# Attention scores of two batches on two halves of the array's rows, inside an attention + two-layer kernel

## The chip, the cores and the metric

The kernel runs on one core of one Trainium2 chip. The core has TensorE (PE in the views, its weight loads are PEld), VectorE (DVE), ScalarE (ACT), GpSimd (POOL) and SyncE (SP, which issues the DMAs here). The metric is the device time of one execution in microseconds (us), as the median of several executions; less is better. All matrix inputs arrive in HBM; the program is one launch.

## The reference, cut to what matters

```python
batch, n_heads, seq, head_dim = 4, 8, 576, 64
# attention, per batch and head
scores = matmul(q, k.T) / 8                       # 576 x 576
cum    = cumsum(maximum(s, 0))                    # one number per key / query
scores = where(causal, -1e9, scores + minimum(-(cum[query] - cum[key]), 0))
attn   = exp(scores - max) / (sum + 1e-9)
x      = attn @ v                                 # 2304 tokens x 512
# layer 1: (x @ w_a) * (x @ w_b) @ w_out          # d_ff 1536
# layer 2: relu(x @ w_in) ** 2 @ w_out2           # d_ff 2048
```

Below the diagonal `-(cum[query] - cum[key])` is never above zero, so the minimum changes nothing there, and the term in `cum[query]` is the same for a whole row, which the softmax removes. What the kernel adds to a score is therefore `cum[key]` alone. The weights are 64-bit floats, which the kernel takes apart into 32-bit parts itself.

## The kernel before, in words

The program first lists its operations and then orders them itself. `Plan.order` (line 148) is a list scheduler: for each engine it holds the operations whose inputs are planned to be there, takes the one that can start first in planned time, and of several the one with the lowest rank (stream, then the order in which they were listed). Costs are written beside each operation, a lateness per engine is added to its result (`LATE`, line 81), and a tile of a tag with few buffers waits in planned time until one is free. What comes out is a fixed order for each engine; on the chip each engine takes its instructions in that order and waits on semaphores. So an operation that is late holds everything behind it on its engine.

Streams in use here: `first` (attention of batch 0), `moe` (layer 1), `next` (attention of batch 1, listed among layer 1's steps from step `TURN` on), `att` (attention of batches 2 and 3), `late` and `fill` (40 dummy matmuls named `glow`, which the planner puts where TensorE would idle; a bank's first matmul may also get a few dummy ones, `idle`, shown as `st<-warm`).

Attention of a head (`softmax`, line 586): the 576 queries are five blocks of 96 or 120 rows; with the causal mask the scores of a head are six pieces of 96, 216, 336, 456, 288 and 288 columns (the last block's 576 keys are cut in two). `banks` (line 499) puts these six into four PSUM banks, and each bank is one planned TensorE operation. In batches 0 and 1 (`WHOLE = 2`) a piece is one plain 32-bit product, contracted over 65 rows: 64 rows of the head, and row 64 that holds ones in the queries' tile and `cum` of that head in the keys' tile, so that the sum comes along in the same product:

```python
both = ((tq[: D + 1, qc], tk[: D + 1, ks]),)
cost += 4 * kn / 2.4 + 13
```

The trace shows two matmul records for each such product. In batch 0 the causal mask is added by a small bf16 product (`tri`) into the same bank. Then for each piece DVE reduces to the row's maximum (`neg`), ACT takes the exponential (`e`) and frees the bank. After both heads of a pair `weigh` (line 669) transposes the weights on TensorE (`pt`), copies them, and multiplies by the values (`av`): there the two heads of a pair lie in two halves of the array's columns (`"tile_position": (0, h * D)`, line 719), and the calls go head 0, head 1 by turns.

Banks: the tag `s` has 2 buffers and serves scores; in batch 0 the third and fourth bank of a head come from the tag `mm` (3 buffers), which layer 1 uses for its products (`ab`, `py`).

Loads: `load_first` (line 436) brings the keys and queries of a head into rows 0 to 63 of two tiles (tags `T2k` and `T2q`, 2 buffers each), `prep_first` (line 533) then loads `cum` of the head into row 64 by a small DMA and scales the queries by 1/8. At the start `cum` is made by DVE (maximum, scan), and its rounded part `ch` and remainder `cl` are written to HBM (`cd`) for batches 2 and 3. Those batches use other operands (`prep`, line 547), a piece there is two products in the faster 32-bit format of the array (`F32R`).

Around this: layer 1 on tokens 0 to 511 (chunk 0) needs batch 0 alone, its steps run beside the attention of batch 1, and at the same time its weights are loaded and taken apart (`split_w`, `words`, `decode`: tiles `roomxh`, `roomxl`, `words`, `wh`, `wl`) and written back to HBM (`wlab`, `wlo`).

Of the kernel before, what the change touches and what calls it, by code (L numbers as in the profile page):

```python
# [263 lines left out]
def attention_moe_moe(tc, q, k, v, s, w_a, w_b, w_out, w_in2, w_out2, out):  # L264
# [21 lines left out]
    MORE = 3 * NF1  # L286
    TURN = 4
    LF1 = 6
# [244 lines left out]
    def prep_first(b, p):  # L533

        load_values(b, p)
        heads = []
        for hh in (2 * p, 2 * p + 1):
            if (b, hh) not in first_k:
                load_first(b, hh)
            tk = first_k[b, hh]  # L540
            dma(tk[D : D + 1].part("c"), cum[b * H + hh : b * H + hh + 1], 2)
            tq = first_q[hh % 2]
            scaled(S, tq[:D].part("x"))
            heads.append((tq, tk))
        return heads
# [40 lines left out]
    def softmax(b, p, h, head, one):  # L586
# [7 lines left out]
        for blk, (tag, width, off) in places.items():  # L594
            if tag not in tiles:
                tiles[tag] = at([P, -(-width // 32) * 32], F32, tag, 3, f"{tag}{nm}")
            place[blk] = (tiles[tag], off)
        for i, pieces in enumerate(banks):
            ps = mm_bank(f"st{nm}_{i}") if b == 0 and i % 4 > 1 else bank(f"st{nm}_{i}")
            off = 0  # L600
            calls, cost, got = [], 0, []
            for blk, k0, kn in pieces:
                at_, m = kb[blk]
                qc = slice(at_, at_ + m)
                to = ps[:m, off : off + kn]
                diag = at_ >= k0 and at_ + m <= k0 + kn
                ks = slice(k0, k0 + kn)
                if b < WHOLE:
                    tq, tk = head
                    both = ((tq[: D + 1, qc], tk[: D + 1, ks]),)  # L610
                    cost += 4 * kn / 2.4 + 13
                else:
                    t1, t2q, t2k = head
                    both = ((t1[:66, 0, qc], t1[:66, 1, ks]), (t2q[:, qc], t2k[:, ks]))
                    cost += 2 * (kn / 2.4 + 15)
                calls += [("matmul", (to, *ab), {"stop": True}) for ab in both]
                if diag and b < MASKED:
                    tri = mask[:m, EDGE : EDGE + m]
                    calls.append(("matmul", (to[:, kn - m :], plain[:m, :m], tri), {"stop": True}))
                    cost += 70  # L620
                e, eo = place[blk]
                got.append((blk, k0, m, to, kn, diag, e[:m, eo + k0 : eo + k0 + kn]))
                off += kn
            if b < WHOLE:
                ins = [tq.part("x"), tq.part("c"), tk.part("x"), tk.part("c")]
# [5 lines left out]
            for z, (_, _, kw) in enumerate(calls):  # L631
                kw.update(start=z == 0, skip_group_check=z > 0)
            pe(cost, calls, ps, ins)
            if b == 0 and i == 0 and hh in (0, 2):
# [11 lines left out]
            held += got  # L646
            whole = [x for x in held if x[0] != LAST or pieces[0][0] == LAST]
            held = [x for x in held if x not in whole]
            if pieces[0][0] == LAST:
# [19 lines left out]
    def weigh(b, p, places, chunk, u):  # L669
# [6 lines left out]
        for i, keys in enumerate(key_banks):  # L676
            m = kb[keys[0]][1]
            rights = []
            for h, place in enumerate(places):
                ps = bank(f"pt{nm}_{h}_{i}", "t")  # L680
                calls, ins, off, spans = [], [ident], 0, []
                for j in keys:
                    k0, _ = kb[j]
                    c0 = max(k0, g0)
                    for blk in range(j, len(kb)):
                        at_, mq = kb[blk]
                        if g0 <= at_ < g0 + n:
                            e, eo = place[blk]
                            ins += [e.part((blk, x)) for x in ((0, HALF) if blk == LAST else (0,))]
                            col = off + at_ - c0  # L690
# [909 lines left out]
```

## Time and profile before

| | |
|---|---|
| Time, median of 3 executions | 1019.21 us (1017.22 to 1020.49) |
| Profiled execution | 1023.91 us, its span 1022.1 us |
| PE busy | 1002.8 us (98% of the span), 5612 matmul records |
| DVE, ACT, POOL busy | 735.5, 603.9, 322.3 us |
| DMA | 240.58 MB, 235 GB/s on average |
| Granted TensorE clock | 1.00 in nearly every stretch |

Stages, read from the names in the timeline: 0 to 10 us set-up; 10 to 62 us attention of batch 0; 62 to 206 us attention of batch 1 beside layer 1's chunk 0; 206 to 378 us attention of batches 2 and 3 beside layer 1; then layer 1 and layer 2 alone. Matmuls are pipelined: the records' durations contain their latency and overlap, so the price of one is read from the distance between starts, not from its duration.

### The profile page before, as it was taken

How to read it: one execution, taken by the hardware profiler on the slowest of the kernel's cores; microseconds unless marked ns; L12 is line 12 of the kernel's file. 1: busy time of each engine (PE TensorE's matmuls, PEld its weight loads, DVE VectorE, ACT ScalarE, POOL GpSimd, SP SyncE). 2: the span in 40 equal slices, each digit the busy share in tenths (PEclk: the TensorE clock that was granted, in tenths of full speed). 3: DMA queues.
4: the chain of work that ended last, by engine and by line, in shares of the span. 5: the costliest groups of instructions: out<-in, count | busy, mean ns of one | idle time of the engine just before them, and what ended most of it. 6: DMA issues, size and time to landing. Idle time of an engine off the chain costs nothing.

```text
span 1022.1 us, 16764 instructions
## 1 busy us (share of the span) xinstructions
PE 1002.8 (98%) x5612; PEld 867.8 (85%) x5619; DVE 735.5 (72%) x1546; ACT 603.9 (59%) x1373; POOL 322.3 (32%) x293
## 2 busy tenths in 40 slices
PE   9999999999999999999999999999999999999997
PEld 5766777777777778788889999999999999999997
DVE  5878876756677765565697898688767755876566
ACT  6777886565777643343344544487565766657552
POOL 2243134325454622101122323323335212431123
PEclk9999999999999999999999999999999999999999
DMA  7458896558778667857666668499968876678664
GB/s 226 131 157 256 273 288 186 152 150 258 228 199 246 185 212 262 275 183 233 206 207 207 208 206 273 164 336 363 344 219 322 313 260 231 246 273 319 220 233 165
DMA packets 138006, 240.58 MB, mean 235 GB/s; under 512 B 21320, under 2 KB 91072, under 8 KB 137920
## 3 DMA queue, kind: packets, MB, share of 16 engines
q1 hardware_dynamic: 137920, 239.52, 71.1%
q8 instruction: 44, 0.72, 0.3%
q14 instruction: 42, 0.34, 0.1%
HBM read 181.42 MB, written 52.11 MB: 228 GB/s over the span
## 4 chain that ended last, share of the span: by engine, by line
PE 75%; DMA 5%; DVE 2%; SPq 1%; ACT 1%; issue 0%; DVEq 0%; ACTq 0%
PE ab L261 14%; PE pa L261 9%; PE py L261 8%; PE po_0t L261 6%; PE pw L261 5%; PE pc L261 5%; PE wa L261 4%; PE st L261 3%; PE av L261 3%; PE pt L261 3%; PE wc L261 2%; PE pb L261 2%; PE po_2b L261 2%; PE po_1b L261 2%; PE po_0b L261 2%; PE po_3b L261 2%
## 5 line engine op out<-in xcount | busy, mean ns | idle before, releaser
L261 ACT ACTIVATE e<-st,neg 120x336 f32<-120x336 f32 (+2 forms) x192 | 93.5, 492 | 28.5 <-DVE neg L261 26.6
L261 PE MATMUL py<-g,wh 128*128 128x512 f32 x288 | 92.0, 401 | 1.4 <-DVE y L261 1.2
L261 PE MATMUL ab<-xh,wh 128*128 128x512 f32 x192 | 77.4, 403 | 0.0
L261 PE MATMUL ab<-xh,lo 128*128 128x512 f32 x192 | 75.0, 391 | 0.0
L261 PE MATMUL ab<-xl,wh 128*128 128x512 f32 x192 | 75.0, 390 | 0.0
L261 PE MATMUL pt<-ident,e 120*120 120x120 f32 (+2 forms) x480 | 68.0, 268 | 0.8 <-DVE ph L261 0.4
L261 PEld LDWEIGHTS pt<-ident,e 120*120 120x120 f32 (+2 forms) x480 | 51.2, 133 | 20.2 <-issue 9.2
L261 DVE CUSTOM_DVE_ANT_0 st<-st,mask 96x96 f32<-96x96 f32 (+4 forms) x120 | 53.7, 453 | 20.0 <-PE st L261 18.2
L261 PE MATMUL ab<-x,wh 128*128 128x512 f32 x192 | 65.8, 424 | 0.8 <-ACT a L261 0.7
L261 PEld LDWEIGHTS py<-g,wh 128*128 128x128 f32 x288 | 53.3, 190 | 12.6 <-DVE y L261 1.6
L261 PE MATMUL av<-ph,val 120*64 120x240 f32 (+3 forms) x512 | 58.7, 360 | 0.0
L261 PE MATMUL st<-fk,fq 65*120 65x336 f32 (+2 forms) x192 | 56.3, 408 | 1.7 <-ACT e L261 1.7
L261 ACT COPY ph<-pt 120x360 f32<-120x360 f32 (+3 forms) x81 | 36.5, 459 | 35.9 <-PE pt L261 34.8
L261 PE MATMUL py<-g,loo 128*128 128x512 f32 x144 | 56.9, 395 | 0.0
L261 PEld LDWEIGHTS av<-ph,val 120*64 120x64 f32 (+1 forms) x512 | 31.1, 136 | 24.9 <-issue 12.4
L261 DVE COPY ph<-pt 120x360 f32<-120x360 f32 (+3 forms) x79 | 39.8, 514 | 16.2 <-PE pt L261 14.9
L261 DVE TENSOR_TENSOR ab<-ab,a 128x512 f32<-128x512 f32 x36 | 25.2, 701 | 33.3 <-PE ab L261 28.7
L261 PEld LDWEIGHTS ab<-xh,lo 128*128 128x128 f32 x192 | 36.0, 188 | 7.7
L261 ACT COPY a<-ab 128x512 f32<-128x512 f32 x36 | 21.1, 586 | 35.7 <-PE ab L261 35.6
L261 PEld LDWEIGHTS ab<-xh,wh 128*128 128x128 f32 x192 | 36.1, 188 | 6.4 <-issue 0.4
L261 PEld LDWEIGHTS ab<-x,wh 128*128 128x128 f32 x192 | 33.7, 189 | 9.2 <-ACT a L261 1.6
L261 PEld LDWEIGHTS ab<-xl,wh 128*128 128x128 f32 x192 | 36.2, 188 | 5.9
(692 smaller groups left out, 3098.4 us busy)
## 6 DMA issues: line engine op xcount, KB each, us to landing
w<-w2q SPq DMA_DIRECT2D x48, 896.0 KB, 6.7
lo<-wlab SPq DMA_DIRECT2D x36, 512.0 KB, 4.7
w2q<-w2ip SPq DMA_DIRECT2D x48, 256.0 KB, 4.2
w2s<-w2op SPq DMA_DIRECT2D x48, 256.0 KB, 4.6
loo<-wlo SPq DMA_DIRECT2D x24, 384.0 KB, 5.5
w2ir<-in_moe_w_in SPq DMA_DIRECT2D x16, 512.0 KB, 5.7
w2or<-in_moe_w_out SPq DMA_DIRECT2D x16, 512.0 KB, 4.3
ws_0t<-w2s SPq DMA_DIRECT2D x12, 512.0 KB
```

Of the source, the lines that this page charges most:

```text
L261: getattr(eng, method)(*map(real, args), **{k: real(a) for k, a in kw.items()})
```

## The change

A head of batches 0 and 1 is now computed in two turns of two banks each. Queries and keys are loaded twice, into rows 0 to 63 and rows 64 to 127. Of the two banks of a turn, one is computed by rows 0 to 63 of the array and one by rows 64 to 127 (`tile_position (side * 64, 0)`). The last block's keys are cut at 396 in place of 288, so that the two banks of a turn have 396 and 396, and 456 and 432 columns. `cum` is no longer a 65th row: each piece gets a second product, in `F32R`, whose moving operand is `sums` (rounded parts and remainders of `cum` of all 32 heads, in 64 rows, twice) and whose stationary operand is one column of `pick` (ones in the two rows of this head), repeated for all queries. The calls of the two banks are interleaved by their costs. `TURN` goes from 4 to 2.

```diff
-    TURN = 4
+    TURN = 2
 def load_first(b, hh):
-        dma(tk[:D].part("x"), k[b, hh], S * 0.25)
-        dma(tq[:D].part("x"), q[b, hh], S * 0.25)
+        for to, x in ((tk, k), (tq, q)):
+            for r in range(2):
+                dma(to[r * D : r * D + D].part(r), x[b, hh], S * 0.25)
...
-    cum = at([P, S], F32, "kh", 1, "cum")[: B * H]
+    cum = at([P, S], F32, "raw", 2, "cum")[: B * H]
...
-    for t in first_q:
-        gps("memset", S, t[D : D + 1].part("c"), 1.0)
-    ch, cl = (at([P, S], F32R, "raw", 2, z)[: B * H] for z in ("ch", "cl"))
-    act("copy", S, ch, cum)
-    dve("tensor_tensor", S, out=cl, in0=cum, in1=ch.bitcast(F32), op=ALU.subtract, two=True)
-    dma(cd[:, 0, :].part(0), ch.bitcast(F32), 74)
-    dma(cd[:, 1, :].part(1), cl.bitcast(F32), 74)
+    BH = B * H
+    sums = at([P, S], F32R, "kh", 1, "sums")
+    pick = at_const([P, BH], F32R, "pick")
+    picks = at([P, P], F32, "rows", 2, "picks")[:, :BH]
+    dve("tensor_reduce", P, out=picks, in_=ident.rearrange("p (i g) -> p g i", g=BH), op=ALU.add, axis=AX.X)
+    act("copy", BH, pick, picks)
+    for i in (0, 2):
+        copy(S, sums[i * BH : i * BH + BH].part(i), cum)
+    for i in (0, 2):
+        subtract(S, sums[i * BH + BH : i * BH + 2 * BH].part(i + 1), cum, sums[i * BH : i * BH + BH].part(i).bitcast(F32))
+    for z in range(2):
+        dma(cd[:, z, :].part(z), sums[z * BH : z * BH + BH].part(z).bitcast(F32), 74)
...
+    PART = 396
+    both_banks = [
+        [[(1, 0, 216), (LAST, PART, S - PART)], [(LAST, 0, PART)]],
+        [[(3, 0, 456)], [(2, 0, 336), (0, 0, 96)]],
+    ]
 def prep_first(b, p):
-            dma(tk[D : D + 1].part("c"), cum[b * H + hh : b * H + hh + 1], 2)
             tq = first_q[hh % 2]
-            scaled(S, tq[:D].part("x"))
+            scaled(S, tq)
 def softmax(b, p, h, head, one):
-        for i, pieces in enumerate(banks):
-            ps = mm_bank(f"st{nm}_{i}") if b == 0 and i % 4 > 1 else bank(f"st{nm}_{i}")
+        for i, turn in enumerate(both_banks if b < WHOLE else [[x] for x in banks]):
+            pss, queues, tops, got, cost = [], [], [], [], 0
+            for side, pieces in enumerate(turn):
+                ps = mm_bank(...) if b == 0 and (i % 2 if b < WHOLE else i % 4 > 1) else bank(...)
...
-                    both = ((tq[: D + 1, qc], tk[: D + 1, ks]),)
-                    cost += 4 * kn / 2.4 + 13
+                        kw = {"stop": True, "tile_position": (side * D, 0)}
+                        calls.append((4 * kn / 2.4 + 13, ("matmul", (to, tq[r, qc], tk[r, ks]), dict(kw))))
+                        left = pick[r, b * H + hh : b * H + hh + 1].to_broadcast([D, m])
+                        ends.append((kn / 2.4 + 13, ("matmul", (to, left, sums[r, ks]), dict(kw))))
...
+            cost += max(sum(n for n, _ in x) for x in queues) + (130 if b < WHOLE else 0)
+            calls, spent = tops, [0.0] * len(queues)
+            while any(queues):
+                z = min((x for x in range(len(queues)) if queues[x]), key=lambda x: spent[x])
+                n, call = queues[z].pop(0)
+                spent[z] += n
+                calls.append(call)
...
-            pe(cost, calls, ps, ins)
+            pl.add({"PE": (cost, calls, False)}, pss, ins)
```

The mask products of batch 0 (`tops`) stand ahead of a turn's other calls and use all rows of the array, as before.

## Rows read from the trace of the kernel before

**Rows 1.** The page: span, and TensorE's busy time, share, instructions.
```profile
span 1022.1 us, 16764 instructions
PE 1002.8 (98%) x5612; PEld 867.8 (85%) x5619; DVE 735.5 (72%) x1546; ACT 603.9 (59%) x1373; POOL 322.3 (32%) x293
```

**Rows 2.** Busy time by stage: stretch, its length, each engine's busy us, clock, DMA.
```profile
core 0: us, PE busy (x) PEld busy (x) DVE busy (x) ACT busy (x) POOL busy (x), PEclk, DMA share, GB/s
10.00:62.00 52.00, 51.80 (x349) 35.33 (x351) 41.51 (x115) 39.13 (x120) 14.08 (x11) 1.00 0.60 181
62.00:206.00 144.00, 140.65 (x732) 103.15 (x735) 111.67 (x275) 106.79 (x255) 50.67 (x38) 1.00 0.73 224
```

**Rows 3.** Groups of matmuls, 10 to 62 us: dummy matmuls (busy us, mean ns).
```profile
L256 PE MATMUL st<-warm 128*128 128x512 bf16 x7 | 1.8, 379 | 0.0
L261 PE MATMUL glow<-warm 128*128 128x512 bf16 x6 | 1.6, 378 | 0.1
```

**Rows 4.** Timeline of TensorE, first head of batch 0: start, length, operation.
```profile
10.05 0.73 PE L261 MATMUL st<-fk,fq 65*120 65x336 f32 x2
10.62 0.22 PE L261 MATMUL st<-mask,plain 120*120 120x120 bf16 x1
10.68 0.36 PE L261 MATMUL st<-fk,fq 65*96 65x96 f32 x2
...
13.35 0.78 PE L261 MATMUL st<-fk,fq 65*120 65x336 f32 x2
```

**Rows 5.** Timeline of TensorE around a product on column halves.
```profile
22.20 0.21 PE L261 MATMUL st<-mask,plain 96*96 96x96 bf16 x1
22.33 1.40 PE L261 MATMUL av<-ph,val 96*64 96x336 f32 x12
23.66 0.63 PE L261 MATMUL pt<-ident,e 120*120 120x120 f32 x4
24.12 0.53 PE L261 MATMUL st<-fk,fq 65*120 65x216 f32 x2
```

**Rows 6.** Instructions of tiles st and av: weight loads, ns min/median/max.
```profile
L261 PEld LDWEIGHTS st<-fk,fq x192: 161/183/186, 9.8 to 205.5; 65*120 65x120 f32 x160, 65*96 65x96 f32 x32
...
L261 PEld LDWEIGHTS av<-ph,val x512: 132/137/139, 22.3 to 377.7; 120*64 120x64 f32 x128, 96*64 96x64 f32 x43
```

**Rows 7.** Chain that ended last, in order of time: start, length, what.
```profile
166.08 4.38 DMA roomxh<-in_moe_w_out
...
171.16 0.62 ACT e L261 x2
...
171.82 1.11 PE st L261 x4
...
188.23 0.72 PE pt L261 x7
...
475.21 16.32 PE ab L261 x72
```

**Rows 8.** Waits of TensorE and its weight loads, 62 to 206 us.
```profile
PE st L261 <- ACT e L261: 1.7, 2, 0.9
...
PEld st L261 <- ACT e L261: 2.9, 3, 1.3
```

**Rows 9.** DMA issues: operation, count, KB each, median us to landing.
```profile
fk<-in_k SPq DMA_DIRECT2D x16, 144.0 KB, 3.6
```

**Rows 10.** Busy time in a 20 us stretch, columns as in rows 2.
```profile
120.00:140.00 20.00, 19.02 (x91) 13.63 (x91) 15.52 (x35) 14.28 (x32) 3.23 (x3) 1.00 0.98 306
```

**Rows 11.** Timeline of the start, all engines.
```profile
2.71 6.21 PE L261 MATMUL glow<-warm 128*128 128x512 bf16 x18
...
3.42 1.35 DVE L261 TENSOR_TENSOR_SCAN cum<-spos 32x576 f32<-32x576 f32 x1
...
5.35 0.65 ACT L261 CAST ch<-cum 32x576 fp32r<-32x576 f32 x1
...
6.03 0.75 DVE L261 TENSOR_TENSOR cl<-cum,ch 32x576 fp32r<-32x576 f32 x1 [1.26 <-ACT ch L261]
...
8.76 1.46 PE L256 MATMUL st<-warm 128*128 128x512 bf16 x6
```

More of the change, by code (lines that the diff above doesn't have):

```diff
@@ L597, in softmax @@
             place[blk] = (tiles[tag], off)
-        for i, pieces in enumerate(banks):
-            ps = mm_bank(f"st{nm}_{i}") if b == 0 and i % 4 > 1 else bank(f"st{nm}_{i}")
[L600 to L609, printed above, removed]
-                    both = ((tq[: D + 1, qc], tk[: D + 1, ks]),)
-                    cost += 4 * kn / 2.4 + 13
[L612 to L623, printed above, removed]
@@ new lines, in softmax @@
+        for i, turn in enumerate(both_banks if b < WHOLE else [[x] for x in banks]):
+            pss, queues, tops, got, cost = [], [], [], [], 0
+            for side, pieces in enumerate(turn):
+                ps = mm_bank(f"st{nm}_{i}_{side}") if b == 0 and (i % 2 if b < WHOLE else i % 4 > 1) else bank(f"st{nm}_{i}_{side}")
+                off = 0
+                calls, ends = [], []
+                r = slice(side * D, side * D + D)
+                for blk, k0, kn in pieces:
+                    at_, m = kb[blk]
+                    qc = slice(at_, at_ + m)
+                    to = ps[:m, off : off + kn]
+                    diag = at_ >= k0 and at_ + m <= k0 + kn
+                    ks = slice(k0, k0 + kn)
+                    if diag and b < MASKED:
+                        tri = mask[:m, EDGE : EDGE + m]
+                        tops.append(("matmul", (to[:, kn - m :], plain[:m, :m], tri), {"stop": True}))
+                        cost += 70
+                    if b < WHOLE:
+                        tq, tk = head
+                        kw = {"stop": True, "tile_position": (side * D, 0)}
+                        calls.append((4 * kn / 2.4 + 13, ("matmul", (to, tq[r, qc], tk[r, ks]), dict(kw))))
+                        left = pick[r, b * H + hh : b * H + hh + 1].to_broadcast([D, m])
+                        ends.append((kn / 2.4 + 13, ("matmul", (to, left, sums[r, ks]), dict(kw))))
+                    else:
+                        t1, t2q, t2k = head
+                        for ab in ((t1[:66, 0, qc], t1[:66, 1, ks]), (t2q[:, qc], t2k[:, ks])):
+                            calls.append((kn / 2.4 + 15, ("matmul", (to, *ab), {"stop": True})))
+                    e, eo = place[blk]
+                    got.append((blk, k0, m, to, kn, diag, e[:m, eo + k0 : eo + k0 + kn]))
+                    off += kn
+                pss.append(ps)
+                queues.append([*calls, *ends])
+            cost += max(sum(n for n, _ in x) for x in queues) + (130 if b < WHOLE else 0)
[5 more added lines that the diff above has]
+                calls.append(call)
@@ L624, in softmax @@
             if b < WHOLE:
-                ins = [tq.part("x"), tq.part("c"), tk.part("x"), tk.part("c")]
+                ins = [tq, tk, sums, pick]
             else:
@@ L629, in softmax @@
                 ins += [plain, mask]
-            for z, (_, _, kw) in enumerate(calls):
-                kw.update(start=z == 0, skip_group_check=z > 0)
-            pe(cost, calls, ps, ins)
+            seen = set()
+            for _, args, kw in calls:
+                new = id(args[0].buf) not in seen
+                seen.add(id(args[0].buf))
+                kw.update(start=new, skip_group_check=not new)
+            pl.add({"PE": (cost, calls, False)}, pss, ins)
             if b == 0 and i == 0 and hh in (0, 2):
@@ L646, in softmax @@
             held += got
-            whole = [x for x in held if x[0] != LAST or pieces[0][0] == LAST]
+            done = b < WHOLE or pieces[0][0] == LAST
+            whole = [x for x in held if x[0] != LAST or done]
             held = [x for x in held if x not in whole]
-            if pieces[0][0] == LAST:
+            if any(x[0] == LAST and x[1] for x in whole):
                 dve(
@@ L688, in weigh @@
                             e, eo = place[blk]
-                            ins += [e.part((blk, x)) for x in ((0, HALF) if blk == LAST else (0,))]
+                            ins += [e.part((blk, x)) for x in ((0, PART if b < WHOLE else HALF) if blk == LAST else (0,))]
                             col = off + at_ - c0
```

## The prediction, made before the changed kernel ran

> **What bounds the kernel now.** I read the page first. TensorE is busy 1002.8 of 1022.1 us [rows 1]: whatever shortens its stream can shorten the end, and nothing else has a comparable share. A busy record holds latency, though, so next I read the busy times by stage [rows 2]. From 10 to 62 us TensorE is busy 51.80 of 52 us, DVE 41.51, ACT 39.13; from 62 to 206 us it is 140.65 of 144, DVE 111.67, ACT 106.79. Neither stage is filled entirely with useful work. In the first, 13 dummy matmuls stand in the stream [rows 3]; at 0.216 us from start to start (1.46 us for six less the last one's latency, [rows 11]) that is 2.8 us of planned slack. In the second, 3.35 us are idle, and the chain of waits shows why it isn't TensorE alone there: a weight's DMA, 4.38 us, ends into ACT's queue, behind it stand two exponentials, and for these a score product waits [rows 7]. The granted clock is 1.00 (the level of 2.4 GHz) in both stages [rows 2].
>
> **What a head costs now.** The first head's first score starts at 10.05 us and the next head's at 13.35 [rows 4]: 3.30 us, of which five mask products take 0.06 each (10.62 to 10.68). The rest is 3.00 us for 1680 columns. The first piece's 336 columns take 0.57 us, that is 1.70 ns a column; 1680 of those are 2.86, the rest is changes between pieces.
>
> **What a head costs afterwards.** If the two halves run side by side, a turn lasts as long as its longer bank: 396 and 456 columns, 852 x 1.70 = 1.45 us. The second product of each piece is in the format that 72 products of 512 columns in 16.32 us show [rows 7]: 0.227 us each, 0.44 ns a column, 852 x 0.44 = 0.38 us. Sum 1.83 us.
>
> Going into halves and back is not free. The trace has one such change, the `av` products on column halves [rows 5]. The mask product before them occupies 0.13 us instead of 0.06 (22.20 to 22.33), +0.07. The twelve last 1.33 us (22.33 to 23.66); four of 336, four of 240 and four of 120 columns at two cycles each are 2.32 us one by one and 1.16 side by side, so +0.17. The four transposes behind them take 0.46 us (23.66 to 24.12) where seven in a row take 0.72, that is 0.41 for four: +0.05. One excursion costs 0.29 us. For scores I add 0.05, since the first weight load is not hidden and a score's takes 183 ns against 137 [rows 6]: 0.34 us, twice per head, 0.68. The new head is then 1.83 + 0.68 = 2.51 us, 0.49 less, and 16 heads give 7.8 us of TensorE. The five masks stay as they are.
>
> For row halves this trace shows neither the side-by-side run nor the price of the change. The bounds: no excursion cost at all, 1.17 us saved per head, 18.7 us in all; no overlap at all, 1680 x (1.70 + 0.44) = 3.60 plus 0.68, that is 4.28 us, +1.28 per head, +20.5 us. I take the value of the nearest row, the column halves, where the overlap is whole.
>
> The Trainium skill ("TensorE: Matmul & The Clock Gate", Part 3: Packing small matmuls) reports 3.07x for four row tiles. No run here shows it; an estimate from that page would be (1 - 1/3.07)/(1 - 1/4) = 0.90 of the possible overlap, hence 2.01 us in place of 1.83 and about 5 us of TensorE instead of 7.8.
>
> **What of that reaches the end.** *Batch 0* (3.9 us saved): the 39 us of ACT and 41.5 of DVE would fill 81% and 86% of the shorter stage; both queues are in order, so some of it turns into dummy matmuls. I count 80%, 3.1 us. *Batch 1* (3.9 us): here waits for weights and exponentials stand in the chain; I count 55%, 2.1 us. Bounds for both: all, and a loss of a microsecond, since the planner will order everything anew and the order of the rest can come out a little worse.
>
> **Start.** Scores no longer wait for the small DMA of `cum` but for `sums`: scan ends at 4.77, then copies at 0.65 (one on ACT, one on DVE) and two subtractions at 0.75 [rows 11], about 7 us. The queries' second half is issued two DMA issues later than now and lands in time for that. What really sets the first score is the planned row of dummies, 18 up to 8.76 and six more [rows 11]; by the costs written in the code the small DMA ends 2.6 us after the scan (issue 0.5, lateness 2.0 and 0.1), copy and two subtractions 2.2, so one dummy less. I take 0.3 us gain; bounds 0 (loads and sums are there before the last dummy ends) and 3 (10.05 less 7). DVE and ACT have some 2 us more to do there, while they wait for loads anyway.
>
> **DMA and queues.** Each head has four loads of 144 KB [rows 9] instead of two plus the small one: +1 issue on SP, +288 KB. For batch 0 the DMA share is 0.60 [rows 2], which hides it. For batch 1 it is 8 x 288 KB = 2.36 MB, and from 120 to 140 us the engines are at 0.98 with 306 GB/s [rows 10]: 7.7 us of transfer if none of it finds room, 0 if the earlier start by `TURN` moves it to free stretches. Behind these issues on SP stand the weights, behind these ACT [rows 7]. I count 0.5 us, near the low end, since the share over the whole stage is 0.73. The `neg` and `e` work has the same number of instructions and columns; scaling the queries over 128 rows takes as long as over 64. `sums` holds the tag `kh` until the last score of batch 1, about as long as the query tiles hold theirs, so the next batch's preparation loses at most one copy, hidden behind layer 1.
>
> **Sum.** -3.1 - 2.1 - 0.3 + 0.5 = -5.0 us. On the profiled execution that is 1023.9 to 1018.9; that execution lay 4.7 us above the median, so on the median of 1019.2 it is **1014.2 us**, -0.5%. Its own range, from the conversion factors: 1010 to 1018.
>
> **Rivals.**
>
> *The passes of one product block the other half (13%).* Each score product has two records. If TensorE starts them strictly in program order, the second pass of one bank holds up the first of the other. With 0.85 ns a column and pass, turn 1 (216 | 396, 180, then the `cum` products) comes to 1.04 us, turn 2 (456 | 336, 96, then those) to 1.32: 2.36 + 0.68 = 3.04 per head, +0.04, and 16 heads give +0.6: no change, 1019 to 1020. Against it speaks the `av` run: in that order its twelve would need 1.44 us of streaming and more than 1.6 with the change of mode, and they took 1.33 [rows 5]; but its neighbours have equal lengths, the score banks don't. The Trainium skill ("TensorE: Matmul & The Clock Gate", Part 3: Packing small matmuls) says that matmuls start and end strictly in program order, which is this rival; for column halves the trace disagrees, with 1.33 us.
>
> *The halves run one after the other (7%).* The slower side: +20.5 us as worked out above, 1036 to 1040. It decides at the share of overlap: 3.60 serial, 1.83 perfect, and a head breaks even at 3.00 - 0.68 = 2.32, so 72% of the possible overlap must be there. For it: no row half in this trace, and two halves now write through the same columns into two banks. Against it: whole overlap on column halves.
>
> *Two banks at a time make TensorE wait (12%).* In batch 1 both banks of `s` go to one turn; it can start only when both are freed, where before one bank sufficed. Now 5 waits on `e`, 4.6 us [rows 8], among 32 bank openings. If all 16 turns waited 0.92 us (that mean), 14.7 us would replace 4.6: +10.1, less the 5.0, 1024. At half of that no change. Against it: TensorE has layer 1's products to do meanwhile, and the planner knows of the two banks.
>
> *The extra loads delay the weights (7%).* All 7.7 us exposed, less 5.0 + 0.5: about 1021.5, no change or a little slower.
>
> *More comes through (9%).* All of 7.8 us plus a start 2 us earlier, or cheaper excursions on rows: 1003 to 1010.
>
> The forecast keeps 52%.
>
> **How the numbers follow.** A measurement of this kernel tells about 0.3% from no change, 3.1 us: faster is below 1016.1, slower above 1022.3. Faster: 0.09 + 0.45 of the forecast's 0.52 = 0.54, +0.02 from the other cases at their good ends: 0.56. Same: 0.06 of the forecast, 0.10 of the blocked passes, 0.05 of the waits, 0.03 of the loads: 0.24. Slower: 0.07 + 0.07 + 0.04 + 0.02: 0.20. The range 1005.5 to 1024 leaves out the serial case (0.07), half of the slow waits and loads (0.06) and the best end (0.04).
>
> **What would show it.** In the first heads of batch 0: score records on two halves starting a few ns apart; a distance from a head's first score to the next head's of 2.8 us instead of 3.3; 0.13 us ahead of a turn. Batch 0's end near 58 instead of 62 us, and batch 1's near 200 instead of 206. Waits of `st` for `e` not much above 4.6 us. Wrong it would be if score starts follow each other by a whole pass, if the stage 62 to 206 keeps its length while its DMA share rises, or if the saved time reappears as dummies.

## The result: 1% slower, with the products as fast as forecast

| | before | changed |
|---|---|---|
| Median, executions of one comparison (4 each) | 1018.95 us | 1029.80 us (1027.68 to 1032.00) |
| Ratio | 1 | 1.0107 [1.0080, 1.0134] |
| Profiled execution, span | 1023.91, 1022.1 us | 1029.86, 1027.9 us |

The forecast was 1014.2 us and the range ended at 1024. The profiled execution of before that the prediction rests on lay 4.7 us above its median; below, stages are therefore compared with a second profile of the same kernel, of span 1020.8 us (the control among the experiments). That execution, of 1022.54 us, lay 3.3 us above its own median too, and the changed one at its median, so this pair of profiles shows 7.1 of the 10.9 us between the medians.

**The page of the changed kernel**, first lines: span, busy us, share, instructions.

```profile
span 1027.9 us, 17043 instructions
PE 1003.2 (98%) x5751; PEld 870.2 (85%) x5751; DVE 742.1 (72%) x1551; ACT 595.5 (58%) x1360; POOL 338.7 (33%) x303
```

TensorE is as busy as in [rows 1], although its products became cheaper: something else fills it. Timeline of TensorE of the changed kernel, first head of batch 0 (start, length, operation):

```profile
9.57 0.27 PE L261 MATMUL st<-mask,plain 120*120 120x120 bf16 x2
9.77 0.93 PE L261 MATMUL st<-fk,fq 64*120 64x216 f32 x5
10.24 0.64 PE L261 MATMUL st<-sums,pick 64*120 64x396 f32 x1
...
10.82 0.36 PE L261 MATMUL st<-mask,plain 120*120 120x120 bf16 x3
11.11 1.02 PE L261 MATMUL st<-fk,fq 64*120 64x456 f32 x4
...
12.28 1.25 PE L261 MATMUL glow<-warm 128*128 128x512 bf16 x5
13.37 0.27 PE L261 MATMUL st<-mask,plain 120*120 120x120 bf16 x2
```

The halves run side by side: in the records the first score products of turn 1 start at 9.774 and 9.781 us. The head takes 9.57 to 12.28, 2.71 us with its five masks, where it took 3.30 [rows 4]; the prediction had 2.51 + 0.30 = 2.81. But behind the head stand five dummies, and the next head begins at 13.37, 3.80 us after the first. Dummy matmuls of the changed kernel, 10 to 62 us and then 62 to 206 us (busy us, mean ns | idle time before):

```profile
L261 PE MATMUL glow<-warm 128*128 128x512 bf16 x23 | 6.1, 380 | 0.0
...
L256 PE MATMUL st<-warm 128*128 128x512 bf16 x8 | 2.1, 379 | 0.0
...
L256 PE MATMUL av<-warm 128*128 128x512 bf16 x1 | 0.4, 381 | 0.0
...
L256 PE MATMUL py<-warm 128*128 128x512 bf16 x24 | 5.5, 379 | 0.3 <-ACT a L261 0.3
L256 PE MATMUL st<-warm 128*128 128x512 bf16 x9 | 2.9, 457 | 2.9 <-ACT e L261 2.9
```

From 62 to 206 us the second profile of before has these:

```profile
L261 PE MATMUL glow<-warm 128*128 128x512 bf16 x10 | 3.1, 380 | 0.1
...
L256 PE MATMUL py<-warm 128*128 128x512 bf16 x2 | 0.6, 386 | 0.0
```

So 12 became 33 there. The 33 are all of the kind that the planner writes ahead of a bank's first product where its own plan leaves TensorE idle for more than 400 ns (`GAP`): a part of the lost time stands in the written order itself.

Busy times of the changed kernel by stage (columns as in [rows 2]):

```profile
10.00:62.00 52.00, 48.01 (x387) 34.95 (x387) 41.63 (x107) 37.24 (x118) 12.63 (x9) 1.00 0.71 216
62.00:206.00 144.00, 140.07 (x802) 103.90 (x800) 113.87 (x275) 99.51 (x239) 54.91 (x41) 0.99 0.76 237
```

From 10 to 62 us TensorE is idle for 3.99 us instead of 0.20 [rows 2], and dummies went from 13 [rows 3] to 32, at 0.216 us each 4.1 us more: 7.9 us more of batch 0 are now spent on nothing. That is one of the signs of being wrong that the prediction named. The waits of score products and their weight loads for exponentials, 62 to 206 us, changed kernel (`st` of L256 are dummies ahead of a bank's scores):

```profile
PE st L256 <- ACT e L261: 2.9, 2, 2.4
...
PEld st L261 <- ACT e L261: 1.2, 2, 0.9
```

And in the second profile of before:

```profile
PE st L261 <- ACT e L261: 0.5, 1, 0.5
```

TensorE itself stood 2.9 us for exponentials, where it stood 1.7 in [rows 8] and 0.5 here, and its longest stop grew from 0.9 to 2.36 us. (The 4.6 us of [rows 8] are no measure of that: at 132.04 and 171.82 us a product and its weight load wait side by side, and both are counted.) The longest stop goes back to a weight's load; timeline of the changed kernel, and its busy times just after:

```profile
136.28 0.69 ACT L261 ACTIVATE words<-words 128x512 f32<-128x512 f32 x1 [1.75 <-DMA words<-in_moe_w_a]
...
139.72 0.60 ACT L261 ACTIVATE e<-st,neg 120x396 f32<-120x396 f32 x1
...
139.89 1.44 PE L256 MATMUL st<-warm 128*128 128x512 bf16 x3 [2.36 <-ACT e L261]
...
140.00:145.00 5.00, 5.00 (x20) 2.55 (x19) 4.37 (x11) 2.74 (x7) 1.29 (x1) 0.69 1.01 315
```

ACT stood 1.75 us for `words`, the exponentials stood behind that, TensorE waited for them, and from 140 to 145 us the granted clock was 0.69 (a mean; 1.00 is the level of 2.4 GHz, 0.50 that of 1.2).

Where the time was lost is seen at four marks: the first product of layer 1 (`ab`), the last score of batch 1, the first product of layer 2 (`wa`), the end. Groups of the tiles, durations and first to last start, second profile of before:

```profile
L261 PE MATMUL st<-fk,fq x192: 244/406/643, 10.2 to 203.6; 65*120 65x288 f32 x64, 65*120 65x336 f32 x32, 65*96 65x96 f32 x32, 65*120 65x216 f32 x32
...
L261 PE MATMUL ab<-x,wh x192: 387/395/752, 64.5 to 227.0; 128*128 128x512 f32 x192
...
L261 PE MATMUL wa<-b11hx,wh x24: 333/334/346, 505.0 to 638.4; 128*128 128x384 f32 x24
```

The changed kernel:

```profile
L261 PE MATMUL st<-fk,fq x192: 242/441/1112, 9.8 to 211.4; 64*120 64x216 f32 x32, 64*120 64x396 f32 x32, 64*120 64x180 f32 x32, 64*120 64x456 f32 x32
...
L261 PE MATMUL ab<-x,wh x192: 387/389/499, 63.3 to 225.0; 128*128 128x512 f32 x192
...
L261 PE MATMUL wa<-b11hx,wh x24: 333/334/346, 512.5 to 650.6; 128*128 128x384 f32 x24
```

Batch 0 ends 1.2 us earlier, batch 1 7.8 later, layer 1 7.5 later, and the end is 7.1 later. In this pair all of the loss arises before 212 us, while these scores are computed. One pair of executions places it only roughly: in the first profile of before the first `wa` starts at 510.4 us, 5.4 later than in the second, though the ends are 1.3 apart.

The chain of waits names what is late. Of the changed kernel, 182 to 225 us (start, length, what):

```profile
186.02 1.32 SPq L261
...
187.39 2.73 DMA fq<-in_q
...
190.23 0.68 ACT fq L261
190.91 0.33 ACT ph L261
...
191.29 0.93 PE pt L261 x7
```

The queries' second load is issued late on SP and lands at 190.12; ACT scales them; the eviction `ph` stands behind the scaling in ACT's queue, though it needs no query; and TensorE's transposes wait for the eviction, 0.6 us. In [rows 7] no load of queries stood in the chain. In batch 0 the same happens on DVE, at a higher price (timeline of the changed kernel):

```profile
53.38 1.13 DVE L261 TENSOR_SCALAR fq<-fq 128x576 f32<-128x576 f32 x1 [1.58 <-DMA fq<-in_q]
...
55.14 0.48 DVE L261 COPY ph<-pt 120x360 f32<-120x360 f32 x1
...
55.68 0.63 PE L261 MATMUL pt<-ident,e 120*120 120x120 f32 x4 [1.66 <-DVE ph L261]
```

TensorE stands 1.66 us here, and 1.56 us at 40.08 behind the scaling of 39.15: together 3.2 of its 3.99 idle us from 10 to 62 us. The tile of the queries, changed kernel: its loads and scalings, what the engines waited for before them, and who waited (us, times):

```profile
L261 SPq DMA_DIRECT2D fq<-in_q x32: 465/594/1325, 2.4 to 187.4; - x32
L261 ACT ACTIVATE fq<-fq x11: 667/684/688, 5.9 to 190.2; 128x576 f32<-128x576 f32 x11
...
  DMA fq<-in_q: 8.2, 8
```

And in the second profile of before:

```profile
L261 SPq DMA_DIRECT2D fq<-in_q x16: 471/588/799, 1.8 to 179.3; - x16
L261 ACT ACTIVATE fq<-fq x13: 669/685/695, 4.7 to 183.9; 64x576 f32<-64x576 f32 x13
...
  DMA fq<-in_q: 3.2, 4
```

Engines stood for 8.2 us instead of 3.2 at the head of their queues for a load of queries. This sum alone does not rank the kernels: among the runs below it is 7.4 us at 1016.44, 13.0 at 1025.14 and 17.6 at 1029.83. From the release of a tile (last score of the head two before) to the end of the scaling, heads 2 to 7 of batch 0 took 6.6, 7.3, 6.0, 4.1, 5.8, 4.7 us before (mean 5.7) and 6.8, 10.1, 7.4, 7.7, 6.4, 7.3 (7.6) now. The first score of these heads starts another 0.9 to 5.9 us after the end of the scaling now, so what a late scaling holds is mostly not the head's own scores.

### The profile page after: what moved, and what is told of

Read it like the earlier page. It is cut to its first block, busy times and chain, and to the rows that moved or that the text cites. A ratio compares the mean times of both kernels' runs of the same rounds, so it can differ in the third digit from the quotient of the medians.

```text
span 1027.9 us, 17043 instructions
## 1 busy us (share of the span) xinstructions
PE 1003.2 (98%) x5751; PEld 870.2 (85%) x5751; DVE 742.1 (72%) x1551; ACT 595.5 (58%) x1360; POOL 338.7 (33%) x303
## 4 chain that ended last, share of the span: by engine, by line
PE 68%; DMA 6%; DVE 5%; ACT 2%; issue 1%; SPq 1%; POOL 0%; DVEq 0%; ACTq 0%
PE ab L261 12%; PE pa L261 9%; PE py L261 6%; PE po_0t L261 6%; PE pc L261 4%; PE pw L261 4%; PE wa L261 3%; PE av L261 3%; PE pt L261 3%; PE st L261 3%; PE pb L261 2%; PE po_3b L261 2%; PE po_2b L261 2%; PE po_1b L261 2%; PE wc L261 2%; PE po_0b L261 2%
## 5 line engine op out<-in xcount | busy, mean ns | idle before, releaser
L261 ACT ACTIVATE e<-st,neg 120x336 f32<-120x336 f32 (+4 forms) x192 | 93.3, 491 | 18.0 <-DVE neg L261 15.2
L261 DVE CUSTOM_DVE_ANT_0 st<-st,mask 120x216 f32<-120x216 f32 (+5 forms) x120 | 52.3, 447 | 18.2 <-PE st L261 16.6
L261 ACT COPY ph<-pt 96x336 f32<-96x336 f32 (+3 forms) x83 | 36.7, 455 | 44.2 <-PE pt L261 42.5
L261 PE MATMUL ab<-x,wh 128*128 128x512 f32 x192 | 61.8, 403 | 0.0
L261 DVE COPY ph<-pt 120x360 f32<-120x360 f32 (+3 forms) x77 | 39.6, 519 | 22.2 <-PE pt L261 17.6
L261 DVE TENSOR_REDUCE neg<-st 120x1 f32<-120x396 f32 (+3 forms) x72 | 31.0, 457 | 11.9 <-PE st L261 8.7
```

What stands on the lines that cost most here:

```text
L261: getattr(eng, method)(*map(real, args), **{k: real(a) for k, a in kw.items()})
```

## The experiments

All ratios are to the kernel before, timed beside it on the same chip, with their 95% intervals. The changed kernel's own ratio, 1.0107, is from another comparison than those below, so that a difference of two ratios carries both intervals, some 3 to 4 us. The theories to separate: the two turns of two banks themselves (pairs); the written order, which comes out anew with any changed cost; the reload of queries and keys, by its issues, its order, or its scaling; the planned dummies.

**Control.** The kernel before, once more.

> The kernel before, unchanged, for a second profile and as the measure of what two runs of the same kernel differ by. All theories: same time as before, within 0.3% (3 us). If the first profile of before was an ordinary one, this one agrees with it stage by stage (layer 1's products start at about 64 us, attention of batch 3 ends at about 378, the first product of the last layer-1 chunk at about 510); if the first one lost some 5 us somewhere, this one shows where.

0.9992 [0.9977, 1.0007], 1019.28 us: the unit of what follows.

### Parts of the change

**Changed kernel, old `TURN`.**

```diff
-    TURN = 2
+    TURN = 4
```

> The changed kernel with TURN back at 4, all else as changed. Theory 1 (the loss is in the score products' new form: two banks an operation, so the order written by the planner holds idle time where it had none): as slow as the changed kernel or slower, ratio to before 1.010 to 1.016. Theory 2 (the loss comes from TURN = 2, which moves batch 1's attention in front of layer 1's weights): the loss goes, ratio 0.994 to 1.001.

1.0146 [1.0111, 1.0181], 1036.18 us.

**Kernel before, new `TURN`.**

```diff
-    TURN = 4
+    TURN = 2
```

> The kernel before with TURN = 2, all else as before. Theory 1: TURN alone is worth little, ratio 0.998 to 1.006. Theory 2: it carries the loss, ratio 1.008 to 1.013.

1.0039 [1.0018, 1.0059], 1023.95 us. The smaller `TURN` hurts the old products, and the new ones are no worse with it (1.0107 against 1.0146, the intervals overlap); it isn't the cause of the loss.

**Pairs of banks alone**: the kernel before with two banks in one operation and the new cut at 396, but full rows, the sum as 65th row, one load per tile, `TURN = 4`.

```diff
-        for i, pieces in enumerate(banks):
+        for i, turn in enumerate(both_banks if b < WHOLE else [[x] for x in banks]):
...
```

> The kernel before with one part of the change alone: two banks of a head in one operation, with the changed pieces (cut at 396), but on all rows of the array with the 65-row product, single loads, cum as a row, TURN = 4. TensorE's work is that of before. Theory 1: this is where the loss sits; without the cheaper products it is larger than in the changed kernel: ratio 1.012 to 1.022, with more dummy matmuls and idle TensorE in batches 0 and 1. Theory 3 (the doubled loads and the longer-held tiles cost the time, not the pairs): ratio 0.998 to 1.004.

1.0114 [1.0080, 1.0148], 1032.45 us: without halves and without doubled loads the pairs, as this order has them, already cost 1.1%. Yet score products have no wait for an exponential from 62 to 206 us in its trace, so it isn't the mechanism of the third rival. Its engines wait for the queries' load instead (tile of the queries, as above):

```profile
  DMA fq<-in_q: 13.9, 8
```

The pairs are not all that differs in this profile. A load of queries issued at 13.63 us took 7.77 us, TensorE stood 1.60 us for the scaling behind it, and the granted clock was then 0.67, 0.50 and 0.55 in the stretches from 22 to 26, 30 and 34 us; over batch 0:

```profile
10.00:62.00 52.00, 49.57 (x290) 33.47 (x294) 38.75 (x107) 36.32 (x110) 14.79 (x12) 0.90 0.65 186
```

How much of the 1.1% the lower clock makes is not known.

### What cheaper scores are worth, and what a new order costs

**Cheap scores, one bank at a time**: the kernel before, with each 32-bit score product of batches 0 and 1 replaced by two bf16 products on constants and one real product of 8 columns, planned at their own cost. The scores of these batches are left out.

```diff
-                    both = ((tq[: D + 1, qc], tk[: D + 1, ks]),)
-                    cost += 4 * kn / 2.4 + 13
+                    both = ((warm[:, :m], warm[:, :kn]),) * 2
+                    cost += 2 * (kn / 2.4 + 13) + 60
...
```

> The kernel before, one bank an operation as before, but the 65-row score product of batches 0 and 1 replaced by two cheap bf16 products on constants and one real product of 8 columns: the scores are left out, so the output is not the reference's. TensorE has about 1.1 us a head less to do, some 17 us in all, more than twice what the change saves, with no pairs of banks. Theory 1a (the pairs of banks eat a saving that would otherwise come through): ratio to before 0.984 to 0.992, 8 to 17 us faster. Theory 1b (TensorE's time in these two batches is worth little in an order in which ACT and DVE are planned full; the saved time becomes dummy matmuls): ratio 0.996 to 1.004, and the dummies and idle time of TensorE grow by 12 to 17 us.

1.0070 [1.0044, 1.0095], 1027.85 us, outside both expectations: slower, although TensorE has less to do and pairs, halves and doubled loads are all absent.

**The same products, planned at the old cost**, so that every engine keeps the written order of before.

```diff
-                    cost += 2 * (kn / 2.4 + 13) + 60
+                    cost += 4 * kn / 2.4 + 13
```

> b1_one_bank_cheap once more (score products of batches 0 and 1 replaced by cheaper ones, so the scores are left out), but planned with the old cost, so that every engine's written order is that of the kernel before, instruction by instruction; TensorE has some 17 us less to do. Theory A (TensorE's time in these batches is worth something, and what made b1 and the changed kernel slow is that a changed cost makes the planner write another, worse order): ratio 0.984 to 0.994. Theory B (these batches are held by loads, ACT and DVE, TensorE's time there is worth nothing in any order): ratio 0.997 to 1.002, TensorE idle instead, some 17 us more.

0.9964 [0.9946, 0.9981], 1016.44 us, between the two expectations. The two kernels issue the same work but for some 15 dummies that the planner adds to the first; what differs is the order, and it costs 1.0070 - 0.9964, 10.8 us. That includes a lower granted clock: 0.91 from 140 to 180 us in the first, where this one had 1.00. What TensorE saves in the second is less than its edit suggests. Timeline of its first head:

```profile
9.18 0.45 PE L261 MATMUL st<-warm 128*120 128x336 bf16 x2
9.46 0.28 PE L261 MATMUL st<-fk,fq 65*120 65x8 f32 x2
9.60 0.24 PE L261 MATMUL st<-mask,plain 120*120 120x120 bf16 x1
...
12.04 0.44 PE L261 MATMUL st<-warm 128*120 128x336 bf16 x2
```

2.86 us from head to head instead of 3.30, 0.44 each, 7.0 us if all 16 heads save as the first does. The forecast had 7.8 us for the change, which by its first head (2.71 for 3.30) saves 9.4. Of these 7.0 us, 3.7 [1.9, 5.5] reach the end, 53% (27 to 79%).

**Another planned constant**, exponentials at 130 ns above their columns, in the changed kernel and in the one before. Nothing that is computed changes.

```diff
-                    "activation", kn + 360, ee.part((blk, k0)), to, AF.Exp, ...
+                    "activation", kn + 130, ee.part((blk, k0)), to, AF.Exp, ...
```

> The changed kernel with one planning cost changed: an exponential is planned with 130 in place of 360 columns on top of its own, which is what the trace shows (0.54 us from start to start for 336 columns; the planner has 0.73). The instructions are the same, their order differs. Theory 1b: ACT is no longer planned full, so batch 0 is planned shorter and the saving comes through: ratio 0.993 to 1.001. Theory 1a: the pairs still hold their banks, ratio 1.006 to 1.012.

1.0059 [1.0035, 1.0083], 1025.14 us.

> The same planning cost in the kernel before, as the control of b2_after_exp. Theory 1b as far as it is about the change alone: TensorE is full already, nothing to gain, ratio 0.998 to 1.006. If it gains as much as b2 does against the changed kernel, the planner's cost is a matter of its own.

1.0064 [1.0041, 1.0087], 1026.18 us. One constant of the planner moves the old kernel by +6.5 us and the changed one by -4.9 (1.0059 against 1.0107).

**Fewer dummies** in the changed kernel: 18 instead of 40, none put into gaps, and not the six ahead of head 2's first bank.

```diff
-    GAP = 400.0
+    GAP = 4.0e9
-    FILL = 40
+    FILL = 18
...
-            if b == 0 and i == 0 and hh in (0, 2):
+            if b == 0 and i == 0 and hh == 0:
```

> The changed kernel without dummy matmuls after the first score (18 dummies at the start and the six ahead of the first bank are left). If the dummies themselves take the time that the products saved (they stand in TensorE's queue ahead of work that could run): 5 to 10 us faster than the changed kernel, ratio to before 1.000 to 1.006. If TensorE would wait there anyway for banks, exponentials or copies: as slow as the changed kernel, ratio 1.008 to 1.014, with the time as idle TensorE instead, and a lower granted clock in places if the idle stretches are long.

1.0086 [1.0065, 1.0107], 1029.84 us, as long as the changed kernel: the dummies seem to fill time that is lost anyway. Without them the granted clock was 0.988 to 0.992 over an execution, where it was 0.998 to 0.999, so what the missing dummies gave back and what the clock took are not told apart.

**The turn planned at its measured price**: 330 ns instead of 130 for the change of mode.

```diff
-(130 if b < WHOLE else 0)
+(330 if b < WHOLE else 0)
```

> The changed kernel with one planning cost changed: a turn's change of mode is planned with 330 ns in place of 130, which is what the trace shows for a turn (1.25 us from the last mask product to the end of turn 1, against 1.01 planned). If TensorE's queue runs late against the plan for this reason and its waits come from that: 2 to 5 us faster than the changed kernel, ratio to before 1.005 to 1.009. If only the order matters, whatever the cost: anything between 1.004 and 1.014, without a sign that the waits of score products got shorter.

1.0091 [1.0052, 1.0131], 1029.83 us: not told apart from the changed kernel, with twice its waits for loads of queries:

```profile
  DMA fq<-in_q: 17.6, 13
```

### The reload

**No reload**: queries and keys of the first two heads are loaded and scaled, and all 16 heads use them; the other loads and scalings are left out.

```diff
-            if (b, hh) not in first_k:
-                load_first(b, hh)
-            tk = first_k[b, hh]
+            tk = first_k[0, hh % 2]
             tq = first_q[hh % 2]
-            scaled(S, tq)
+            if b == 0 and hh < 2:
+                scaled(S, tq)
```

> The changed kernel with queries and keys of two heads loaded and scaled once and used for all sixteen heads of batches 0 and 1 (the other fourteen heads' loads and scalings are left out, so the output is not the reference's). Theory C (with TensorE's stream shorter, the reload of the two query tiles, load, scaling and its place in the queues, becomes the chain from head to head): batch 0 ends 4 us or more earlier than in the changed kernel (first layer-1 product before 60 us instead of 63.3), ratio to before 0.990 to 1.000. If the pairs of banks and the order are what holds: ratio 1.004 to 1.011, batch 0 as long as before.

0.9925 [0.9890, 0.9959], 1014.22 us: 18.5 us below the changed kernel (1.0107 - 0.9925), and about the time that was forecast. Its batch 0:

```profile
8.70:57.50 48.80, 47.69 (x393) 35.96 (x396) 39.30 (x110) 37.73 (x117) 12.05 (x10) 1.00 0.50 160
```

First score at 8.7, first `ab` at 57.5: 48.8 us, where before needed 54.3 and the changed kernel 53.5.

**The same in the kernel before** (the small load of `cum` goes with it).

> The same in the kernel before, as the control of c2 (loads, the small DMA of cum and scalings of fourteen heads left out). Theory C: TensorE's stream bounds batch 0 there, so little is gained: first layer-1 product at 62 to 64 us, ratio 0.996 to 1.003. If a new order alone costs some 5 us, as in a2 and b3: ratio 1.002 to 1.006.

0.9998 [0.9979, 1.0017], 1019.74 us. In the kernel before the reload shows no cost that can be told, in the changed one it shows 18.5 us; both runs also have a written order of their own.

**One issue per tile**: the source is repeated, so that one DMA of 288 KB fills both halves.

```diff
-            for r in range(2):
-                dma(to[r * D : r * D + D].part(r), x[b, hh], S * 0.25)
+            both = x[b, hh].rearrange("(o d) s -> o d s", o=1).to_broadcast([2, D, S])
+            dma(to, both, S * 0.5)
```

> The changed kernel, but keys and queries of a head come by one DMA issue each that fills both halves of the tile (the source repeated), 288 KB, in place of two issues of 144 KB; bytes as before, half the issues on SP. Theory (the queries' arrival is the chain, and the four issues of a head on SP delay it): the last load of a head lands about 1.2 us earlier, 16 heads, half of them on the chain: 0.6 to 1.2% less than the changed kernel, 1018 to 1024. Rival (bytes or the reload as such): same as the changed kernel, 1027 to 1032. Rival (any new written order moves the time by several us either way): no relation to the waits for the queries.

1.1316 [1.1281, 1.1352], 1156.68 us: far outside all its expectations, because this form of DMA is slow here. Its chain of waits, 10 to 140 us:

```profile
6.60 21.72 DMA fq<-in_q
...
42.99 20.04 DMA fq<-in_q
```

About 20 us from issue to landing, where [rows 9] has 3.6 for 144 KB. So the run says nothing on the number of issues, but it shows the loop: from 10 to 140 us loads of queries make up 74% of the chain.

**Queries ahead of keys**, and both edits together.

```diff
-        for to, x in ((tk, k), (tq, q)):
+        for to, x in ((tq, q), (tk, k)):
```

> The changed kernel with the queries' two loads issued before the keys' two. The scaling follows the queries alone. Theory (the chain runs load of queries, scaling, score): scaling starts about 1.2 us earlier per head, the keys land while it runs: 3 to 8 us less, 1022 to 1027. Rival (the load of both matters, or the release of the tiles): same, 1028 to 1032.

1.0080 [1.0059, 1.0102], 1029.98 us: the order of the four issues is worth nothing that can be told.

> Both: one issue for each tile, queries first. By the theory the sum of the two gains, 1015 to 1022, and the waits of ACT and DVE for the queries' load fall from 8.2 us to about 3, as in the kernel before. By the rivals 1027 to 1032.

1.1307 [1.1274, 1.1339], 1154.96 us, as slow as the repeated source alone.

**All loads, but scaling for the first two heads only** (the other 14 heads' queries stay unscaled).

```diff
-            scaled(S, tq)
+            if b == 0 and hh < 2:
+                scaled(S, tq)
```

> The changed kernel with all loads, but the queries scaled for the first two heads only; the scaling of the other 14 is left out (their scores come out 8 times too large). If the scaling, waiting for a load in the queues of ACT and DVE and holding what stands behind it, is what the reload costs, most of the 18 us that the kernel without reloads gained come back: 1012 to 1018. If it is the loads on SP and their transfers, little: 1026 to 1032.

0.9979 [0.9950, 1.0009], 1016.49 us: 13.0 of the 18.5 us come back with 14 short operations gone (9.1 us of ACT's and DVE's time in the changed kernel) and every load still there. The remaining 5.5 us are hardly more than the two intervals leave open. Nor are the loads harmless here: in this run's profile TensorE stood 2.16 us for a load of queries before 20.64 us, with a granted clock of 0.72 from 20 to 26. Its ten executions differ by that clock: six of 1014 to 1017 us had 0.999 to 1.000 over the whole, four of 1021 to 1024 had 0.993 to 0.997.

**Scaling on GpSimd** (first two heads excepted).

```diff
-            scaled(S, tq)
+            if b == 0 and hh < 2:
+                scaled(S, tq)
+            else:
+                gps("tensor_scalar", S, tq, tq, D**-0.5, None, op0=ALU.mult)
```

> The changed kernel with the scaling of the queries on GpSimd in place of ACT or DVE (the first two heads excepted), everything else computed as in the changed kernel. GpSimd is busy 14 of 52 us in batch 0 and one such operation takes some 1.4 us there. Theory (the scaling waits for a late load at the head of ACT's or DVE's queue and holds evictions and exponentials behind it): nothing urgent stands behind it on GpSimd, so most of the 12 us that leaving the scaling out gained come back: 1018 to 1023, and no wait of ACT or DVE for the queries' load is left. Rival (the scaling's length on the way load, scaling, score counts, wherever it runs): 0.75 to 0.95 us more for each of 14 heads, half of them on the chain, 5 to 7 us slower than the changed kernel: 1033 to 1037. Rival (only the written order): no relation, 1022 to 1032.

1.0036 [1.0011, 1.0061], 1025.02 us: 7.2 us better than the changed kernel, above what the theory expected and within the range of the rival by which only the order counts. The tile of the queries in this run:

```profile
L261 POOL TENSOR_SCALAR fq<-fq x14: 1643/1652/2239, 20.8 to 191.4; 128x576 f32<-128x576 f32 x14
...
  POOL fq L261: 30.3, 10
```

The operation takes 1.65 us instead of 0.68, and release to scaled takes 9.9, 12.8, 9.1, 12.2, 8.1, 9.8 us for heads 2 to 7 (mean 10.3, against 7.6). The loop became longer and the kernel faster. That speaks for the place of the waiting operation, at the head of a queue with evictions and exponentials behind it, and against its length; it is not shown by it, since 7.2 us lie within what a new order alone is worth (4 to 11 us in these runs). On GpSimd it waited ten times, 30.3 us in all, for its load, and no eviction or exponential stood behind it. The chain still holds it:

```profile
27.35 5.39 DMA fq<-in_q
...
32.91 1.65 POOL fq L261
```

**That and the exponentials' constant.**

```diff
+                gps("tensor_scalar", S, tq, tq, D**-0.5, None, op0=ALU.mult)
...
+                    "activation", kn + 130, ee.part((blk, k0)), to, AF.Exp, ...
```

> The same with the exponentials planned at 130 ns above their columns in place of 360, which alone brought the changed kernel from 1030 to 1025. If the two gains are independent: 1013 to 1018, a version ahead of the kernel before. If the gain of either was only a better written order: 1018 to 1030.

1.0070 [1.0043, 1.0096], 1027.87 us: the gains don't add, and the constant, worth 4.9 us in the changed kernel, is worth nothing here, as expected if its gain was that of an order. No version that computes the whole was found ahead of the kernel before. More buffers for queries and keys, which would take the release out of the loop, were not tried.

## Why the prediction was wrong

**What bounds the kernel: too simple.** TensorE's 98% was read as the bound, with a discount for dummies. The dummies and 0.20 us of idle time said how often TensorE lacked work, not how near the other queues were to being late.

**A head's price: right.** 2.71 us with masks against 2.81 forecast; two changes of mode cost 2.71 - 0.30 - 1.83 = 0.58 instead of 0.68. Both rivals on the product, blocked passes (3.04 + 0.30) and serial halves (4.28), are refuted by the same row.

**Conversion, "80%" and "55%": not refuted.** In the old order about as much saved TensorE time gave 53% (27 to 79), 3.7 us, where the prediction had 5.2 of 7.8 (67%).

**"A loss of a microsecond, since the planner will order everything anew": this is the step that failed, together with the 0.5 us for loads and queues.** A new order of the same work cost 10.8 us (cheap scores), and other harmless edits 4.0 (`TURN`) and 6.5 us (a constant). The bound of 1 us had no row behind it; I had none that showed a second order, and should have widened the range for that. The planner's own length of its plan (`self.length` in `Plan.order`, which follows from the kernel file alone) would have given one: 998.5 us before and 999.9 changed. The saving of the products was gone in the plan already, and 9 us more were lost against it on the chip (measured less planned, 20.7 us before and 29.9 now).

**"Scaling the queries over 128 rows takes as long as over 64", "the DMA share hides it": true as durations (0.68 us, [rows 9]'s loads), wrong as cost.** The four issues occupy SP for 2.4 us (12.20 to 14.59 for head 2) where the two and the small one took 1.8, and the scaling waits for the queries' second half in the in-order queues of ACT and DVE. Leaving out scaling is worth 13.0 us in the changed kernel, leaving out the reload 18.5, and in the old one the reload is worth nothing, each in an order of its own. The prediction asked what stands behind the issues on SP (weights) and not what stands behind the waiting scaling on ACT and DVE (evictions, hence TensorE's transposes): 3.8 us of TensorE's stops in the changed kernel's profile are traced to it.

**Rivals.** *Two banks at a time*: its price (+10.1 us, 1024) was nearest, and pairs alone measured +11.6; but its mechanism, TensorE waiting for exponentials, shows only in part: 2.9 us of its stops against 1.7, where the rival had 14.7 against 4.6, and that price counted stops twice. *Extra loads delay the weights*: not refuted. TensorE's longest stop in batch 1 goes back to a weight's load; whether the extra loads made it late was not tested, and [rows 7] has such a stop without them. *More comes through* (1003 to 1010): no run came there. That the kernel without the reload took 1014.22 us, the forecast's number, is luck: it leaves out work that the forecast had in it.

**What stays open.** Order and reload can't be separated fully: every edit to the reload also changes the written order, by amounts of the same size. The planned length says what an order had written in: it is 1010.4 us for the pairs alone, 991.1 without the scaling and 994.9 without the reload. So the pairs alone lost in the plan (11.9 us) about what they lost on the chip, and 8.8 of the 13.0 us and 4.9 of the 18.5 stand in the plan too. Shown is that leaving out the reload gives the changed kernel more than any change of order gave here, and the old one nothing, and that evictions behind a waiting scaling stopped TensorE. Not shown is how much of the loss that place in the queue makes, with the order, the weights' loads and the clock beside it. The doubling alone, one bank at a time, was not run.

## What to carry to other kernels

Where a program writes out its own order, price a new order by itself: change a harmless constant and see how far the time goes, and compare the planned lengths first; here that is 4 to 11 us, about as much as the edit was worth or more. For each operation that waits for a load, ask what stands behind it in its engine's queue: behind a scaling that waited 1.58 us for its load stood an eviction, and TensorE stopped 1.66 us for that. A saving on the busiest engine is best tested first with stand-in products of the new price in the old order; that one run said 3.7 us, not 7.

## What the chip showed that was not expected

Two row halves overlap fully with unequal lengths: their first products start 7 ns apart, and the second pass of one doesn't hold up the other, since turn 1 takes 1.05 us (9.77 to 10.82) for 396 columns at 1.70 + 0.44 ns, 0.85 us, plus the change of mode; one after the other the two would take 792 columns, 1.69 us. A load whose source is repeated over two groups of partitions took about 20 us for 288 KB; how it is spread over the DMA engines was not looked into. The granted clock fell after some stops of TensorE and not after others: 0.69 from 140 to 145 us after 2.36 us in the changed kernel, but 1.00 after its stops of 1.56 and 1.66 us in batch 0. A kernel's profile must be judged against its median: the first of before lay 4.7 us above it, the second 3.3.
